# GpSimd issues the load of Wb's second quarter before its first masking product instead of after it

## The chip, the cores and the metric

The kernel runs on one core of a Trainium2 chip. The metric is the device time of one execution in microseconds (us); lower is better. A core has five engines that run their own instruction streams and wait for each other through semaphores: TensorE (PE in the profile, its weight loads PEld), VectorE (DVE), ScalarE (ACT), GpSimd (POOL) and SyncE (SP, which here only issues transfers). Data moves between the chip's memory and the on-chip buffer (SBUF) by DMA; a DMA is issued by an instruction of ACT, GpSimd or SP and then runs beside the engines. Matmul results land in PSUM, which TensorE writes and DVE and ACT read here.

## What is computed

A state-space layer (Mamba-2 in its chunked form) feeds a bilinear feed-forward layer. Batch 4, 8 heads, 768 tokens, head dimension 32, state dimension 16, all in float32 at the interface:

```python
# per batch and head, with state carried over chunks of tokens
cum = cumsum(log a)
M   = (C @ B.T) * exp(cum_i - cum_j) * causal
y   = M @ x + exp(cum_i) * (C @ state)
state = exp(sum log a) * state + sum_j exp(cum_end - cum_j) * outer(B_j, x_j)
# then, with the heads side by side: X is 3072 x 256
out = ((X @ w_a) * (X @ w_b)) @ w_out      # w_a, w_b: 256 x 1536, w_out: 1536 x 256
```

## The kernel before

The tokens are cut into 6 blocks of 128. A *pair* is two batches of one block, so there are 12 pairs (0 to 11); pairs 0 and 1 are block 0, pairs 2 and 3 block 1, and so on. One pair goes through these steps:

- B and C are scaled by decay factors (`scale_bc`, the product is at L319), giving `bm` and `cm` in float16. For pair 0, DVE does both. For pair 1, GpSimd scales B (L833) and DVE scales C (L837).
- `bm` and `cm` are transposed on TensorE, and `scores` (L427) multiplies them into four PSUM banks.
- `mask` multiplies each bank by the causal 0/1 mask and writes float16 tiles `t`. It has two forms. On DVE it is one product that reads PSUM directly (L467). With `by_pool=True`, ACT copies the bank to an SBUF tile `tmp` (L464) and GpSimd multiplies `tmp` by the mask (L465), since GpSimd works from SBUF here.
- `pv_u` (L487) multiplies the masked scores with x; ACT or DVE copy the result to float16 `X2T`.
- The feed-forward layer works on `X2T` in units of two 128-column slices of the weights: `aps` (with Wa) and `bps` (with Wb), matmuls at L667 and L682; ACT copies `aps` out (`asb`, L694), DVE multiplies it with `bps` into `hk` (L701); `ops` (L716) multiplies `hk` with Wo.

The order of instructions is written out by hand (`tc.manual_schedule()`): the order of the calls from L812 on is the order on each engine. An engine runs its own instructions in that order.

The weights are cast from float32 to float16 on the way in, by DMAs that GpSimd issues. Wa arrives in two halves, and the first half of Wb in two quarters of its own tiles, so that the first units can begin early: `load_w0(0, 0)` and `load_w0(1, 0)` bring Wa's first half and Wb's first quarter (L176, called at L232 and L233), `load_w0(1, 1)` brings Wb's second quarter (called at L859), and `load_w(1)` both second halves (L168). x of pairs 0 and 1 (`load_x0`, L151), B, C and x of pair 2 (L143), and Wo (L184) are issued by GpSimd as well. All of them share one DMA queue (q0 in the profile); SP's and ACT's transfers have queues of their own. Wb's second quarter is first read by `unit_mm(0, 1, Wb, (1,), ...)` at L898, as slices 3 to 5 of `w_of`.

GpSimd's order around the change, from the start, is: x of pair 0, Wa's first half, Wb's first quarter, x of pair 1, B of pair 1 scaled (L833), the mask of pair 0's `product0(1, 1)` (L836), Wb's second quarter, Wa's and Wb's second halves, the mask of pair 1's `product(1, 3)` (L862), three small products for the state (L864 to L866), B and C of pair 2, Wo, x of pair 2.

DVE's order beside it is: the masks of pair 0's `product0(0, 0)` and `product0(0, 1)`, C of pair 1 scaled (L837), the mask of pair 0's `product0(1, 0)`, a scan, a reciprocal, then the masks of pair 1.

TensorE's order is: scores of pair 0, warm-up matmuls, pair 1's B transposed, `pv_u(0, 0)` (heads 0 to 3 of pair 0), pair 1's C transposed, `pv_u(0, 1)` (heads 4 to 7, which read the masks of `product0(1, 0)` and `product0(1, 1)`), the scores of pair 1, and from L872 on the feed-forward units.

Of the kernel before, what the change touches and what calls it, by code (L numbers as in the profile page):

```python
# [28 lines left out]
def kernel(  # L29
# [102 lines left out]
    def by_token(t_):  # L132
        return t_.rearrange("p h r n -> p (h r n)").rearrange("p (t h n) -> p t h n", t=2, h=H)
# [31 lines left out]
    def load_w(half):  # L165
        c = slice(half * KC, (half + 1) * KC)
        return [
            nc.gpsimd.dma_start(W[half], src.rearrange("(f p) e -> p f e", p=128)[:, :, c])  # L168
            for W, src in ((Wa, moe_w_a), (Wb, moe_w_b))
        ]  # L170

    def load_w0(which, part):
        W, src = ((Wa, moe_w_a), (Wb, moe_w_b))[which]
        w = (KC, KC // 2)[which]
        t_ = W[0][part] if which else W[0]
        nc.gpsimd.dma_start(t_, src.rearrange("(f p) e -> p f e", p=128)[:, :, part * w : (part + 1) * w])  # L176
# [109 lines left out]
    def of_pair(f, blk, bp):  # L286
        if blk * NBP >= P0:
            return flat(f, blk, blk + 1).rearrange("p (b r h) -> p b r h", b=NBP, r=2)[:, bp]
        return f[:, blk, :, bp]
# [16 lines left out]
    def scale_bc(p, which, eng, factor=None):  # L306
        blk, bp = divmod(p, NBP)
        name, f = (("bm", fB), ("cm", fC))[which]
        raw = by_token(pair_in[p][which]) if p >= P0 else pair_in[p][which].rearrange("p h r n -> p r h n")
        if p >= P0 and which:  # L310
            eng.tensor_tensor(  # L311
                out=planes[p % 2][:, 4:6].rearrange("p t (h n) -> p t h n", n=N),
                in0=raw,
                in1=of_pair(f, blk, bp).unsqueeze(3).broadcast_to((128, 2, H, N)),
                op=ALU.mult,
            )
            return
        m_ = mid.tile([128, 2, H, N], f16, name=name, tag=name)
        eng.tensor_tensor(  # L319
            out=m_,  # L320
            in0=raw,
            in1=(of_pair(f, blk, bp) if factor is None else factor).unsqueeze(3).broadcast_to((128, 2, H, N)),
            op=ALU.mult,
        )
        st.setdefault(p, {})[name] = m_
        if p >= P0:
            dst = planes[p % 2][:, 0:4].rearrange("p (t e) (m f n) -> p t e m f n", e=2, f=2, n=N)
            for e in range(2):
                eng.tensor_copy(dst[:, :, e, :, e], m_.rearrange("p t (m f) n -> p t m f n", f=2)[:, :, :, e])
# [76 lines left out]
    def scores(p):  # L406
        BT, CT = st[p]["BT"], st[p]["CT"]
        st[p]["T1"] = mid.tile([128, H, 2, Q], f16, name="t1", tag="t1")
        for e, bt, m in itertools.product(range(2), range(2), range(4)) if p >= P0 else ():
            rows = slice(32 * m, 32 * m + 32)  # L410
            c0 = (e * 2 + bt) * Q
            nc.tensor.matmul(  # L412
                SC[m][:, c0 : c0 + Q],
                BT[rows, e, bt],
                CT[rows, bt],
                start=True,
                stop=True,
                skip_group_check=True,
                tile_position=(32 * m, 0),
            )  # L420
        for e in range(2) if p < P0 else ():
            for r in range(2):
                for m in range(4):
                    for bt in range(2):
                        rows = slice(32 * m, 32 * m + 32)
                        c0 = (e * 2 + r) * Q
                        nc.tensor.matmul(  # L427
                            SC[m][64 * bt : 64 * bt + 64, c0 : c0 + Q],
                            BT[rows, e, r, bt],
                            CT[rows, bt],  # L430
                            start=True,
                            stop=True,
                            skip_group_check=True,
                            tile_position=(32 * m, 64 * bt),
                        )
# [13 lines left out]
    def product0(m2, e):  # L449

        return (
            st[0]["T1"][:, 4 * m2 : 4 * m2 + 4].rearrange("p (m e) r q -> p e m (r q)", e=2)[:, e],
            (SC0, SC1)[m2][:, :, e * 256 : e * 256 + 256],
        )

    def mask(out_in, by_pool=False, by_token=False):
        o_, i_ = out_in
        if by_token:
            c_ = causal_q.unsqueeze(1).broadcast_to((128, 4, Q))
        else:  # L460
            c_ = causal.rearrange("p r q -> p (r q)").unsqueeze(1).broadcast_to((128, 2, 2 * Q))
        if by_pool:
            tmp = mid.tile([128, *c_.shape[1:]], f32, name="tmp", tag="tmp")
            nc.scalar.copy(tmp, i_)  # L464
            nc.gpsimd.tensor_tensor(out=o_, in0=tmp, in1=c_, op=ALU.mult)  # L465
        else:
            nc.vector.tensor_tensor(out=o_, in0=i_, in1=c_, op=ALU.mult)  # L467
# [363 lines left out]
    warmup(2, SC[3], 128)  # L831
    scores(0)
    scale_bc(1, 0, nc.gpsimd)  # L833
    mask(product0(0, 0))
    mask(product0(0, 1))
    mask(product0(1, 1), by_pool=True)  # L836
# [19 lines left out]
    over_mid(2, NBLK)  # L856
    raw = [lambda bt=bt: nc.scalar.mul(U32[:, 0, bt], st[0]["DS"][bt], XS) for bt in range(2)]
    raw[0]()
    load_w0(1, 1)  # L859
    w1 = load_w(1)  # L860
    scores(1)
    mask(product(1, 3), by_pool=True)  # L862
# [290 lines left out]
```

## Time and profile before

| what | value |
|---|---|
| time, median of 3 runs | 121.41 us (121.41 to 121.86) |
| the profiled execution's own time | 121.82 us |
| its span, first to last instruction | 120.1 us |
| mean granted TensorE clock | 0.997 |
| busy: TensorE | 115.1 us (96%) |
| busy: DVE, ACT, GpSimd | 86.2, 73.7, 60.6 us |

The span is what the profiler sees of the profiled execution; the time holds 1.7 us more around it. Times in the views are counted from the start of the span. A line of the timeline gives start, duration, engine, kernel line, operation, output and inputs, and in brackets for how long the engine was idle before it and what ended that idle time. The chain of work that ended last lists, from the last instruction back, what released what. An engine's busy share is an average over the whole span and says little about the first 25 us, where the change lies.

### The profile page before, as it was taken

Reading aid. Unit: us, or ns where it says so; the run is one execution under the profiler, and the core shown is the slowest. Engines: PE = TensorE matmul, PEld = TensorE weight load, DVE = VectorE, ACT = ScalarE, POOL = GpSimd, SP = SyncE. Lnnn points to the kernel's source line nnn. Section 1 sums busy time; section 2 is a strip of 40 time slices with the busy share of each in tenths; the row PEclk is TensorE's granted clock in tenths of the full one; section 3 lists DMA queues with packets and bytes.
Section 4 is the critical chain, followed back from the end, with each engine's and each line's share of the span. In section 5 each row is a group of like instructions: output and inputs, shape, how many; then the busy total and the mean of one; then the engine's idle time right before and its main releaser. Section 6 shows DMA issues by size and latency. Waiting matters only on the chain.

```text
span 120.1 us, 3705 instructions
## 1 busy us (share of the span) xinstructions
PE 115.1 (96%) x1452; PEld 80.2 (67%) x1452; DVE 86.2 (72%) x169; ACT 73.7 (61%) x151; POOL 60.6 (50%) x105
## 2 busy tenths in 40 slices
PE   5997999999999999999999999999999999999990
PEld 5645899888898888544475464765465684655890
DVE  5988785994989897599975999576899435847100
ACT  0467767676875777887567737645645737566220
POOL 6998997299978532596834992039400000000200
PEclk9999999999999999999999999999999999999998
DMA  3999999958949799579788947879601012010032
GB/s 62 146 162 155 181 202 171 228 95 104 115 79 90 128 175 93 91 123 177 76 110 153 100 167 262 115 83 180 203 0 49 11 40 81 0 49 0 20 111 87
DMA packets 69185, 13.44 MB, mean 112 GB/s; under 512 B 64048, under 2 KB 68912, under 8 KB 69168
## 3 DMA queue, kind: packets, MB, share of 16 engines
q1 hardware_dynamic: 62272, 9.31, 47.2%
q0 software_dynamic: 4368, 3.54, 18.6%
q10 hardware_dynamic: 2528, 0.36, 1.8%
q8 instruction: 11, 0.18, 0.6%
q14 instruction: 6, 0.05, 0.2%
HBM read 11.11 MB, written 3.15 MB: 119 GB/s over the span
## 4 chain that ended last, share of the span: by engine, by line
PE 82%; DMA 7%; POOL 4%; DVE 2%; ACT 1%; issue 1%
PE ops L771 18%; PE aps L746 18%; PE bps L746 17%; PE ops L716 8%; DMA Wo<-in_moe_w_out_dram 7%; PE aps L667 4%; PE bps L667 4%; PE SC L239 4%; PE SC L412 2%; PE SC L473 2%; POOL bn L143 1%; DVE t L467 1%; POOL cn L143 1%; POOL t L465 1%; PE SC L566 1%
## 5 line engine op out<-in xcount | busy, mean ns | idle before, releaser
L694 ACT COPY asb<-aps 128x512 f32<-128x512 f32 x72 | 41.4, 588 | 13.9 <-PE aps L746 9.6
L756 DVE TENSOR_TENSOR hkb<-bps,asb 128x512 f16<-128x512 f32 x48 | 32.3, 688 | 12.8 <-ACT asb L694 11.8
L746 PE MATMUL aps<-XB,Wa 128*128 128x512 f16 x96 | 28.6, 379 | 0.0
L746 PE MATMUL bps<-XB,Wb 128*128 128x512 f16 x96 | 28.5, 379 | 0.0
L771 PE MATMUL ops<-Wo,hkb 128*128 128x256 f16 (+1 forms) x204 | 22.5, 267 | 0.0
L771 PEld LDWEIGHTS <-hkb 128*128 128x128 f16 x204 | 18.5, 98 | 3.1
L467 DVE TENSOR_TENSOR t<-SC,causal_q 128x512 f16<-128x512 f32 x27 | 17.2, 681 | 3.1 <-PE SC L412 3.1
L701 DVE TENSOR_TENSOR hk<-bps,asb 128x512 f16<-128x512 f32 x24 | 15.9, 684 | 4.5 <-PE bps L667 2.2
L746 PEld LDWEIGHTS <-Wb 128*128 128x128 f16 x96 | 9.9, 103 | 10.9
L746 PEld LDWEIGHTS <-Wa 128*128 128x128 f16 x96 | 9.7, 103 | 9.1 <-issue 0.2
L783 ACT ACTIVATE osb<-ops 128x256 f32<-128x256 f32 (+1 forms) x16 | 6.0, 378 | 14.2 <-PE ops L771 14.1
L785 POOL DMA_DIRECT2D out_dram<-osb x1 | 0.6, 647 | 26.8 <-ACT osb L783 26.8
L667 PE MATMUL bps<-X2T,Wb 128*128 128x256 f16 x96 | 13.6, 273 | 0.0
L716 PE MATMUL ops<-Wo,hk 128*128 128x256 f16 x96 | 11.7, 273 | 0.1
L667 PE MATMUL aps<-X2T,Wa 128*128 128x256 f16 x80 | 11.4, 273 | 0.0
L311 POOL TENSOR_TENSOR planes<-cn,fC 128x256 f16<-128x256 f32 x8 | 5.0, 622 | 11.2 <-DMA cn<-in_C_dram 11.0
L667 PEld LDWEIGHTS <-Wb 128*128 128x128 f16 x96 | 9.7, 103 | 0.6
L716 PEld LDWEIGHTS <-hk 128*128 128x128 f16 x96 | 8.9, 98 | 1.7 <-issue 0.3
L319 POOL TENSOR_TENSOR bm<-bn,fB 128x256 f16<-128x256 f32 x11 | 6.8, 622 | 3.9 <-DMA bn<-in_B_dram 2.9
L667 PEld LDWEIGHTS <-Wa 128*128 128x128 f16 x80 | 8.1, 103 | 0.6
L304 POOL TENSOR_SCALAR x<-xn 128x512 f16<-128x512 f32 x5 | 7.5, 1492 | 1.5 <-DMA xn<-in_x_dram 1.3
L467 DVE TENSOR_TENSOR t<-SC,causal 128x512 f16<-128x512 f32 x12 | 7.7, 683 | 0.7 <-PE SC L427 0.7
(115 smaller groups left out, 130.0 us busy)
## 6 DMA issues: line engine op xcount, KB each, us to landing
out_dram<-osb SPq DMA_DIRECT2D x22, 128.0 KB, 1.8
xn<-in_x_dram SPq DMA_DIRECT2D x6, 256.0 KB, 4.1
cn<-in_C_dram SPq DMA_DIRECT2D x8, 128.0 KB, 4.2
bn<-in_B_dram SPq DMA_DIRECT2D x8, 128.0 KB, 4.6
Wa<-in_moe_w_a_dram POOLq DMA_DIRECT2D x2, 384.0 KB, 6.6
Wo<-in_moe_w_out_dram POOLq DMA_DIRECT2D x2, 384.0 KB, 7.9
xn<-in_x_dram SPq DMA_DIRECT2D x4, 128.0 KB, 3.7
Wb<-in_moe_w_b_dram POOLq DMA_DIRECT2D x2, 192.0 KB, 5.7
```

The costliest lines, as they stand in the source:

```text
L304: eng.tensor_scalar(xo, xi, XS, None, ALU.mult)
L311: eng.tensor_tensor(out=planes[p % 2][:, 4:6].rearrange("p t (h n) -> p t h n", n=N), in0=raw, in1=of_pair(f, blk, bp).unsqueeze(3).broadc ...
L319: eng.tensor_tensor(out=m_, in0=raw, in1=(of_pair(f, blk, bp) if factor is None else factor).unsqueeze(3).broadcast_to((128, 2, H, N)), op ...
L467: nc.vector.tensor_tensor(out=o_, in0=i_, in1=c_, op=ALU.mult)
L667: nc.tensor.matmul(ps[:, kk * 2 * Q : (kk + 1) * 2 * Q], w_of(W, k, f), X2T[:, p, :, f], start=(f == 0), stop=(f == 1), skip_group_check=True,
L694: (nc.vector.tensor_copy if on_dve else nc.scalar.copy)(asb, a_ps)
L701: nc.vector.tensor_tensor(out=s["hk"][:, 2 * k2 : 2 * k2 + 2, :].rearrange("p k q -> p (k q)"), in0=b_ps, in1=asb, op=ALU.mult)
L716: nc.tensor.matmul(o_ps[:, 0:d_model], hk[:, k, bt * Q : (bt + 1) * Q], Wo[:, k, :], start=(k == 0), stop=(k == NK - 1), skip_group_check= ...
L746: nc.tensor.matmul(t_, w_of(W, k, f), XB[:, blk - P0 // NBP, f].rearrange("p t j q -> p (t j q)"), start=(f == 0), stop=(f == 1), skip_gro ...
L756: return lambda: nc.vector.tensor_tensor(out=s["hk"][:, k], in0=ps[1], in1=asb, op=ALU.mult)
L771: nc.tensor.matmul(o_ps[:, 0:w], hk[:, k, c * Q : (c + 1) * Q], Wo[:, k, cs], start=(k == 0), stop=(k == NK - 1), skip_group_check=True,)
L783: nc.scalar.activation(out=o_sb[:, 0:w], in_=o_ps[:, 0:w], func=AF.Copy, scale=1.0 / (YS * YS))
```

## The change

GpSimd's instruction that issues the DMA of Wb's second quarter is moved ahead of GpSimd's first mask. The instructions are the same, and so are the order of the DMAs among themselves and the order on every other engine.

```diff
     scores(0)
     scale_bc(1, 0, nc.gpsimd)
+    load_w0(1, 1)
     mask(product0(0, 0))
     mask(product0(0, 1))
     mask(product0(1, 1), by_pool=True)
@@
     raw = [lambda bt=bt: nc.scalar.mul(U32[:, 0, bt], st[0]["DS"][bt], XS) for bt in range(2)]
     raw[0]()
-    load_w0(1, 1)
     w1 = load_w(1)
```

## The prediction

> **What bounds the kernel now.** I read the chain of waits that ended last first, then the timeline of each engine around the place of the change, then the transfers that GpSimd issues. The whole-span shares say that TensorE is busy 96% of the span; the question is therefore where TensorE still waits and what the moved instruction can do to those waits.
>
> The chain, in the stretch from the masks of pair 0 to the arrival of Wo (start, duration, what):
>
> ```profile
> 7.94 0.68 DVE t L467
> 8.62 0.80 DVE cm L319
> 9.42 0.61 DVE t L467
> 10.04 0.04 issue
> 10.08 0.39 PE py L487 x16
> ...
> 11.59 1.15 POOL t L465
> ...
> 16.94 8.62 DMA Wo<-in_moe_w_out_dram
> 25.56 0.04 issue
> 25.60 1.47 PE ops L716 x12
> ```
>
> DVE's last mask of pair 0 releases `pv_u(0, 1)` at 10.08; from there the chain goes through GpSimd's second mask and its issues to Wo, whose landing at 25.56 lets TensorE go on. Behind 25.60 the chain is TensorE to the end.
>
> TensorE's own waits in the first 27 us, after its warm-up has begun, are two short ones:
>
> ```profile
> 10.08 0.30 PE L487 MATMUL py<-t,x 64*32 64x128 f16 x16 [0.31 <-DVE t L467]
> 10.31 0.43 PE L427 MATMUL SC<-ct,bt 32*64 32x128 f16 x32
> 11.08 1.05 PE L682 MATMUL aps<-X2T,Wa 128*128 128x256 f16 x8 [0.34 <-DMA Wa<-in_moe_w_a_dram]
> ```
>
> The second, 0.34 us until Wa's first half lands, is a buffer: whatever makes `pv_u(0, 1)` late by up to 0.34 us costs nothing, since TensorE would stand there anyway. At 25.60 there is a third: TensorE is busy 0.90 us in the stretch from 25 to 26, so it loses about 0.10 us to Wo.
>
> GpSimd around the change:
>
> ```profile
> 7.35 0.62 POOL L319 TENSOR_TENSOR bm<-bn,fB 128x256 f16<-128x256 f32 x1
> 7.98 1.16 POOL L465 TENSOR_TENSOR t<-tmp,causal 128x512 f16<-128x512 f32 x1
> 9.09 0.76 POOL L176 DMA_DIRECT2D Wb<-in_moe_w_b_dram  x1
> 9.84 0.71 POOL L168 DMA_DIRECT2D Wa<-in_moe_w_a_dram  x1
> 10.54 0.72 POOL L168 DMA_DIRECT2D Wb<-in_moe_w_b_dram  x1
> 11.59 1.15 POOL L465 TENSOR_TENSOR t<-tmp,causal 128x512 f16<-128x512 f32 x1 [0.33 <-ACT tmp L464]
> ```
>
> The stream is dense from 7.35 to 11.26, then idle 0.33 us until ACT's copy for the second mask is there.
>
> DVE beside it, the two scalings of C (first pair 0's, then pair 1's) and the product after it:
>
> ```profile
> 5.36 0.42 DVE L319 TENSOR_TENSOR cm<-cn,fps 128x256 f16<-128x256 f32 x1
> ...
> 8.54 0.89 DVE L319 TENSOR_TENSOR cm<-cn,fC 128x256 f16<-128x256 f32 x1
> 9.35 0.68 DVE L467 TENSOR_TENSOR t<-SC,causal 128x512 f16<-128x512 f32 x1
> ```
>
> The reader is to see that the same operation takes 0.42 us at 5.36 and 0.89 us at 8.54, and that it ends at 9.43, 0.29 us behind the end of GpSimd's mask at 9.14. Its 256 elements need little more than that, so the trace looks as if it stood still while GpSimd's mask ran and then did its work. The earlier one ran while GpSimd only issued DMAs.
>
> **The change part by part.**
>
> *The issue goes in front.* GpSimd's `bm` ends at 7.97. An issue that follows a product starts about 0.05 us before the product's shown end (9.14 to 9.09), so this one starts at 7.92; with 0.72 to 0.76 us (the first Wb issue took 0.71) it ends at 8.64 to 8.68. The next product starts 0.01 to 0.06 us behind an issue (7.29 to 7.35 after x), so the first mask can start at 8.65 to 8.74 instead of 7.98, some 0.7 us later. Its input `tmp` is long there: ACT copies it from 7.32 to 7.91.
>
> *Who waits for that mask.* `pv_u(0, 1)` at 10.08 reads both GpSimd's mask and DVE's last one. Undisturbed, the mask ends at 8.74 + 1.16 = 9.90 at the latest, 0.18 us ahead of 10.08. So the delay of 0.7 us lies beside DVE's path, which today ends last. If that cover were gone, the same 0.7 us would stand on the path, less the 0.34 us at 11.08.
>
> *The scaling of C meets the mask differently.* DVE's `cm` can start when its mask ends at 8.62 (the row gives 8.54, as rows overlap by 0.08). The mask now starts at 8.65 to 8.74, so `cm` is first by 0.03 to 0.20 us. Then it is `cm` that runs free and the mask that stands: `cm` takes its 0.34 to 0.42 us and ends at about 8.96 to 9.04, DVE's last mask ends at 9.57 to 9.65 instead of 10.03, and GpSimd's mask runs from there: 8.96 + 1.16 = 10.12, or 10.20 with the later end. `pv_u(0, 1)` then waits for GpSimd instead of DVE and starts at 10.16 to 10.24, which is 0.08 to 0.16 us later. That is what is late next, and TensorE absorbs it at 11.08, inside its 0.34 us. Sum for TensorE: 0. [...]
>
> *DVE's scan* (0.40 us at 9.95, two SBUF inputs) could now meet the mask as well; it would end by about 10.4 to 10.5 against 10.35, and the next DVE mask waits for TensorE's scores until 10.88, so this costs nothing.
>
> *What is queued behind on GpSimd.* One mask and three issues take the same time together. With the mask ending at 10.12 to 10.20, Wa's and Wb's second halves are issued at about 10.1 and 10.85 and done by 11.6, 0.3 us later than now. GpSimd's second mask started at 11.59 when `tmp` was there; with ACT late by 0.08 to 0.16 us as well, it starts at 11.67 to 11.75. The three small products and seven issues behind it (B, C, Wo, the first x of pair 2) shift by 0.1 to 0.2 us. SP's queue and ACT's keep their order; SP's next transfers wait for Wb's second half, which landed at 10.54 + 7.9 = 18.4.
>
> *The transfers.* The order in q0 is unchanged, and the queue is backlogged: Wa's first half was issued at 4.48 and landed at 11.08, Wb's first quarter at 12.0, pair 1's x at about 12.4 and 12.9, Wb's second quarter at 9.09 + 4.7 = 13.8. TensorE first needs that quarter at 14.69, so 0.9 us of slack hides it already, and an earlier landing is worth nothing by itself. Only a gap in the queue could be closed by an earlier issue. There is one candidate, in the quarter from 11.25 to 11.5:
>
> ```profile
> q0 software_dynamic: 22, 0.02, 53.5%
> ```
>
> The share is 104% in the quarter before and 132% in the one behind, so at most about 0.2 us of queue time is missing there. Bounds: nothing if the transfers that decide a landing have no gap, and 0.2 us earlier for all that follows, Wo included, if it is closed. I take 0, because landings come 1.3 to 2 us after most of their packets, which points to a few late streams that are backlogged throughout. If Wo does land 0.2 us earlier, TensorE gains its 0.10 us at 25.60. In the other direction the issues of Wa's and Wb's second halves, 0.3 us late, have a backlog of over 2 us ahead of them, and Wo at 16.27 one of 7 to 8.6 us until landing; I cost that at 0, with 0.2 us as the upper bound.
>
> *The sum.* Against the profiled execution: 120.1 us of span, 0 from TensorE at 11.08, between -0.10 and +0.2 at 25.60, taken as 0: 120.1, and with the 1.7 us around it 121.8. That execution stands 0.4 us above the median of the runs shown, so on the median the forecast is 121.4 us, with 121.3 to 121.6 for this case.
>
> **The rivals.**
>
> *The mask gets there first (slower).* The margin of 0.03 to 0.20 us is thin, and GpSimd's start depends on issues while DVE's depends on arrivals and on TensorE's scores, so it can tip. Then `cm`, with its two SBUF inputs, stands until the mask ends, at 8.70 + 1.16 = 9.86, and needs 0.29 us more (10.15); DVE's last mask ends at 10.76 and `pv_u(0, 1)` starts at 10.80, 0.72 us late. TensorE absorbs 0.34, so 0.38 us reach the units; GpSimd's second mask ends at 13.46 instead of 12.74, and pair 1's `pv1`, now at 13.3 to 13.5, just gets it. Of the 0.38, the 0.10 lost to Wo today hide a part: +0.28. If Wo also lands later with its issue, the full 0.72 counts. Middle +0.45: 121.9 us. It passes the 0.5% mark (0.6 us) only if Wo follows its issue. For it speaks the thin margin, against it DVE's earlier row start of 8.54. [...]
>
> *The gap in the queue is closed and the path gets shorter (faster).* With `cm` free and the queue filled, the waits of 0.31, 0.34 and 0.10 us on TensorE are all there is to win: 0.75 at most, and TensorE is bound by Wo's landing, which moves by 0.2. Likely -0.1 to -0.4: 121.2 us. For it speaks the 53.5%, against it the backlog.
>
> *A new wait elsewhere (slower).* The gap on TensorE around 10 us grows, or pair 1's x, which lands at about 12.9 and is needed at 12.94, comes later because Wb's packets now stand closer behind it. Each us there is a us on the path: +0.7 or more, 122.2 us. The shared order of the queue speaks against it.
>
> **How the numbers follow.** Forecast 0.55, mask first 0.28, gap closed 0.10, new wait 0.07. A measurement of this kernel can tell about 0.5% from no change, since its three runs lie 0.4% apart. Slower by more than that: half of the second case and nearly all of the last, 0.14 + 0.06 = 0.20. Faster by more: half of the third, 0.05. The rest, 0.75, is within. The range runs from 121.0 (gap closed, most of its waits won) to 122.1 (mask first with all of its 0.72); what lies outside is some of the last case and the ends of the others, under 0.2. For the likeliest case alone it is 121.3 to 121.6.
>
> **What the profile after would show.** If the steps hold: GpSimd's issue at 7.9 and its mask behind it, DVE's `cm` near 0.42 us instead of 0.89, `pv_u(0, 1)` released by GpSimd's mask at about 10.2, TensorE still standing for Wa until about 11.1, and Wo landing near 25.6. If `cm` keeps 0.89 us or grows to 1.5, and `pv_u(0, 1)` starts near 10.8, the mask was first. If q0's share in the quarter from 11.25 is over 100% and Wo lands before 25.4, the gap was real. The prediction is wrong if TensorE's start of the units moves from 11.08, or Wo's landing by more than 0.3 us, either way.

## The result and the profile after

The changed kernel takes 123.13 us (median of 6, 122.41 to 123.33) against 121.63 us (121.15 to 122.25): ratio 1.012, 95% interval 1.009 to 1.015. It is slower by 1.2%, and outside the range of 121.0 to 122.1. The profiled execution took 123.04 us with a span of 121.3 us, 1.2 us more than before. The ratios here leave out the few executions of the kernel before that lie over 1.5% above its fastest, among them all six whose mean TensorE clock was below 0.99, so they compare with the kernel before at full clock.

The chain of waits of the changed kernel, over the stretch that the prediction showed:

```profile
7.79 0.68 DVE t L467
8.47 1.70 DVE cm L319
10.17 0.61 DVE t L467
10.78 0.04 issue
10.82 0.30 PE py L487 x16
```

DVE's scaling of C (`cm`) stands on it with 1.70 us instead of 0.80. The timelines of GpSimd and of DVE say why (start, duration, engine, line):

```profile
7.93 0.76 POOL L176 DMA_DIRECT2D Wb<-in_moe_w_b_dram  x1
8.71 1.17 POOL L465 TENSOR_TENSOR t<-tmp,causal 128x512 f16<-128x512 f32 x1
```

```profile
8.38 1.78 DVE L319 TENSOR_TENSOR cm<-cn,fC 128x256 f16<-128x256 f32 x1
10.09 0.68 DVE L467 TENSOR_TENSOR t<-SC,causal 128x512 f16<-128x512 f32 x1
```

The issue and the mask stand where the prediction put them. But the scaling, free to start at 8.47 when DVE's mask ends, is done only at 10.16, 0.28 us behind the end of GpSimd's mask at 9.88. The mask won, although its row starts 0.24 us later. TensorE:

```profile
10.22 0.28 PE L378 MATMUL SC<-ident,cm 128*128 128x128 f16 x2 [0.83 <-DVE cm L319]
10.82 0.30 PE L487 MATMUL py<-t,x 64*32 64x128 f16 x16 [0.31 <-DVE t L467]
11.06 0.43 PE L427 MATMUL SC<-ct,bt 32*64 32x128 f16 x32
11.42 1.50 PE L682 MATMUL aps<-X2T,Wa 128*128 128x256 f16 x8
12.71 1.06 PE L667 MATMUL aps<-X2T,Wa 128*128 128x256 f16 x4
...
17.00 1.92 PE L667 MATMUL bps<-X2T,Wb 128*128 128x256 f16 x16
```

and before, behind the eight matmuls at 11.08 that the prediction shows:

```profile
11.97 0.60 PE L667 MATMUL aps<-X2T,Wa 128*128 128x256 f16 x4
...
15.35 1.92 PE L667 MATMUL bps<-X2T,Wb 128*128 128x256 f16 x16
```

The units start at 11.42 instead of 11.08, 0.34 us later, and the wait for Wa is gone. The second loss is in the durations: four matmuls that took 0.60 us now show 1.06, eight that took 1.05 show 1.50. The view by stretches has the reason (length, then PE and its busy time, PEld, DVE, ACT, POOL, then the granted TensorE clock, DMA share, GB/s):

```profile
8.00:11.88 3.88, 2.70 (x99) 1.75 (x100) 3.51 (x6) 2.48 (x10) 3.25 (x4) 1.00 1.48 185
11.88:15.28 3.40, 3.40 (x63) 2.24 (x61) 2.19 (x4) 1.81 (x5) 2.78 (x6) 0.50 1.10 168
15.28:20.00 4.72, 4.72 (x46) 4.43 (x45) 3.98 (x9) 3.26 (x9) 4.72 (x8) 1.00 0.82 152
```

From 11.88 to 15.28, for 3.4 us, TensorE ran at half clock. From the start of the units to the 16 matmuls of `bps` behind them it was 11.08 to 15.35 before and is 11.42 to 17.00 now: 4.27 against 5.58 us, 1.31 us lost.

The account of the two profiled executions: +0.34 for the late start, +1.31 for the clock, -0.17 up to the `ops` matmuls at L716 (23.37 before, 24.85 after), and -0.25 inside these, since the wait for Wo is gone; that is +1.23, and the span grew by 1.2. Wo's second half landed some 6.6 us after its issue, near 24.3, where it had taken 8.6 us and landed at 25.56.

Of the six executions, five had a mean clock of 0.983 to 0.986 (123.04 to 123.33 us). The sixth had 1.000 and took 122.41 us.

### The profile page after: what moved, and what is told of

It reads as the page before. It is cut to its first block, busy times and chain, and to the rows that moved or that the text cites. A ratio compares the mean times of both kernels' runs of the same rounds, so it can differ in the third digit from the quotient of the medians.

```text
span 121.3 us, 3705 instructions
## 1 busy us (share of the span) xinstructions
PE 115.6 (95%) x1452; PEld 80.7 (66%) x1452; DVE 87.3 (72%) x169; ACT 73.5 (61%) x151; POOL 60.3 (50%) x105
## 4 chain that ended last, share of the span: by engine, by line
PE 89%; DVE 5%; DMA 2%; ACT 1%; issue 0%
PE ops L771 18%; PE aps L746 17%; PE bps L746 17%; PE ops L716 9%; PE bps L667 9%; PE aps L667 8%; PE SC L412 2%; PE aps L682 2%; PE SC L473 2%; DMA a_sb<-in_a_dram 2%; DVE t L467 1%; DVE cm L319 1%; PE SC L427 1%; PE SC L487 1%; DVE Pr L246 1%; PE SC L566 1%
## 5 line engine op out<-in xcount | busy, mean ns | idle before, releaser
L694 ACT COPY asb<-aps 128x512 f32<-128x512 f32 x72 | 41.4, 588 | 13.7 <-PE aps L746 9.6
L667 PE MATMUL bps<-X2T,Wb 128*128 128x256 f16 x96 | 14.1, 279 | 0.0
L716 PE MATMUL ops<-Wo,hk 128*128 128x256 f16 x96 | 11.5, 273 | 0.0
L716 PEld LDWEIGHTS <-hk 128*128 128x128 f16 x96 | 8.9, 98 | 1.4
L465 POOL TENSOR_TENSOR t<-tmp,causal_q 128x512 f16<-128x512 f32 x5 | 5.8, 1160 | 5.7 <-ACT tmp L464 5.6
```

What stands on the lines that cost most here:

```text
L667: nc.tensor.matmul(ps[:, kk * 2 * Q : (kk + 1) * 2 * Q], w_of(W, k, f), X2T[:, p, :, f], start=(f == 0), stop=(f == 1), skip_group_check=True,
L694: (nc.vector.tensor_copy if on_dve else nc.scalar.copy)(asb, a_ps)
L716: nc.tensor.matmul(o_ps[:, 0:d_model], hk[:, k, bt * Q : (bt + 1) * Q], Wo[:, k, :], start=(k == 0), stop=(k == NK - 1), skip_group_check= ...
```

## The experiments

The theory after this result has two steps. First, DVE's scaling of C and GpSimd's mask exclude each other, and with the issue in front the mask shuts the scaling out. Second, TensorE, which stands meanwhile, gets a lower clock behind it. The rivals are that the earlier transfer costs the time through the queue, and that the clock fell for another reason. All ratios are against the kernel before, run on the same chip; "low clock" counts executions with a mean clock below 0.99. The tile `pause`, where there is one, is written and not read. The changed kernel itself ran a second time on one chip only, beside the kernels with the late scaling and with the memset ahead of the issue; what it would have measured beside the others is not on record, so ratios from different chips are compared with care.

| run | ratio (95% interval) | low clock |
|---|---|---|
| changed kernel | 1.012 (1.009 to 1.015) | 5 of 6 |
| changed kernel, another chip | 1.011 (1.003 to 1.018) | 1 of 4 |
| changed, scaling reads PSUM | 1.004 (1.001 to 1.008) | 0 of 10 |
| the same, another chip | 1.007 (1.003 to 1.010) | 2 of 10 |
| changed, four more warm-ups | 1.001 (0.999 to 1.004) | 0 of 10 |
| changed, memset behind the issue | 1.002 (0.998 to 1.005) | 0 of 10 |
| changed, short memset behind the issue | 1.008 (1.004 to 1.012) | 0 of 5 |
| changed, memset ahead of the issue | 1.005 (1.001 to 1.010) | 1 of 8 |
| before, two warm-ups less | 1.011 (1.006 to 1.016) | 3 of 4 |
| before, scaling reads PSUM | 1.004 (1.001 to 1.008) | 0 of 10 |
| before, memset ahead of the mask | 1.005 (1.002 to 1.009) | 1 of 10 |
| before, scaling late by a DVE memset | 1.012 (1.005 to 1.019) | 1 of 4 |
| before, two more warm-ups | 0.999 (0.996 to 1.002) | 0 of 12 |
| before itself, beside the last twelve | | 6 of 83 |

### Take the collision away

```diff
-    scale_bc(1, 1, nc.vector)
+    scale_bc(1, 1, nc.vector, v.rearrange("p (r b h) -> p r b h", r=2, b=NBP)[:, :, 1])
```

> The changed kernel, but DVE's scaling of pair 1's C takes its factors from PSUM instead of from the SBUF tile fC, so that it has one SBUF input; nothing else is touched. Theory (the scaling and GpSimd's mask exclude each other, since both read two SBUF operands): the scaling falls from 1.78 us to about 0.42 us and ends near 8.9, the last mask of DVE ends near 9.5, pv_u(0, 1) starts by 10.1, the clock stays at 1.0, and the time is that of before, ratio 0.994 to 1.004. Rival (the earlier transfer itself costs the time, through the queue): the ratio stays at 1.012.

The scaling's factors now come from the PSUM bank `fps`. GpSimd's and DVE's timelines:

```profile
8.71 1.17 POOL L465 TENSOR_TENSOR t<-tmp,causal 128x512 f16<-128x512 f32 x1
```

```profile
8.49 0.41 DVE L319 TENSOR_TENSOR cm<-cn,fps 128x256 f16<-128x256 f32 x1
9.42 0.74 DVE L246 TENSOR_TENSOR_SCAN Pr<-a_sb,zero 32x128 f32<-32x128 f32 x1
```

With one SBUF input the scaling takes 0.41 us beside the same mask, so the second SBUF input is what collided. The scan with its two SBUF inputs now meets the mask instead: 0.74 us instead of 0.40, ending at 10.16, again 0.28 us behind the mask's end at 9.88. The units start at 11.04 and the clock holds in all ten executions. The ratio of 1.004 lies at the edge of what was expected and under 1.012, and something small is left.

In this profile TensorE stood once more:

```profile
13.15 0.21 PE L514 MATMUL SC<-x,bm 64*32 64x64 f16 x3
13.95 0.24 PE L514 MATMUL SC<-x,bm 64*32 64x64 f16 x13 [0.59 <-issue]
```

To see whether that and the 0.4% come from the earlier transfer, the kernel was run again beside the kernel before with the same edit:

> The changed kernel with the scaling's factors from PSUM once more, on the same chip as the kernel before with this edit; the two differ only in the place of the issue. Theory (the earlier transfer is worth nothing and costs nothing): the two ratios agree within 0.3%. Rival (the earlier transfer costs something by itself, which the ratio of 1.004 in the first run of this kernel may show): this one is 0.4% or more above the other. A second thing to see is whether TensorE stands again for about 0.6 us near 13.3 in the state's products, as in the first run; if it does not, that was one execution's.

> The kernel before with DVE's scaling of pair 1's C taking its factors from PSUM, so that it cannot collide with GpSimd's mask. It asks what the collision costs before the change, and, beside the rerun of the changed kernel with the same edit, what the earlier transfer does alone. Theory (a late scaling is absorbed while TensorE waits for Wa, as long as the clock holds): the scaling takes 0.42 instead of 0.89 us, pv_u(0, 1) starts near 9.6 instead of 10.08, the units still start near 11.1, ratio 0.997 to 1.003. Rival (the late scaling is on the path): 0.45 us gained, ratio 0.996 or below.

The ratios are 1.0065 (1.003 to 1.010) and 1.0044 (1.001 to 1.008). They differ by 0.2%, inside their intervals, so an effect of the earlier transfer alone is not shown, in either direction. Read the other way, moving the issue costs 1.1 to 1.2% where the scaling and the mask can collide, and 0.2%, which the noise covers, where they can't: the collision carries the loss. Two of the ten executions behind the 1.0065 had the low clock, so that does not vanish altogether with the collision. The stand in the state's products came back (0.60 us at 13.89), at the same instruction, and 0.35 and 0.25 us of it in two other executions of kernels with the early issue. In the profiles of before and of before with this edit the same 16 matmuls show 0.46 us instead of about 0.25, so a part of it is there too. The profile names nothing that TensorE waits for there. One thing in the traces fits: in both profiles the stand is ahead of the fourth of these matmuls, and TensorE goes on 2.2 to 2.3 us after the one 16 KB packet of the queue that the view names `q8 instruction` (at 13.95 after 11.63 in the first, at 13.89 after a packet between 11.6 and 11.7 in the second). No run tested whether the two belong together, so its cause stays open.

Before with the edit is not faster: the scaling took 0.41 us and `pv_u(0, 1)` started at 9.71, but the units waited until 11.65 for Wa in that execution. Gaining on the scaling was worth nothing there, since Wa landed behind it. That this kernel measured 0.4% slower was not expected, and the profile gives no more than that later landing for it; the 0.4% that is left with the edit in the changed kernel may be the edit's own.

### Keep TensorE busy, or less busy

```diff
     part(1)
-    warmup(2, tcp)
+    warmup(6, tcp)
```

> The changed kernel with four more warm-up matmuls of 512 columns (some 0.22 us each) on TensorE ahead of pv_u(0, 0), in time that TensorE otherwise spends waiting for the scaling of C. Theory (two costs: the late scaling, about 0.35 us at the start of the units, and on top a lower TensorE clock that follows from TensorE's longer standstill): the scaling stays at about 1.7 us, the units still start near 11.4, but the granted clock stays at 1.0 from 12 to 16; ratio 1.003 to 1.008. Rival (the lower clock has another cause than the standstill, or comes by chance): clock about 0.59 from 12 to 16 again, ratio 1.012.

In the changed kernel with this edit the collision is as before (`cm` 1.52 us, from 8.65), and TensorE's timeline starts the units as late as after the change:

```profile
11.42 1.06 PE L682 MATMUL aps<-X2T,Wa 128*128 128x256 f16 x8
12.31 0.60 PE L667 MATMUL aps<-X2T,Wa 128*128 128x256 f16 x4
```

But eight matmuls take 1.06 us, not 1.50; the clock held in all ten executions, and the ratio fell from 1.012 to 1.001 (0.999 to 1.004). Four matmuls that compute nothing took the loss away with the collision left in. By this run the clock is the larger part, and a start of the units that is 0.34 us late costs little by itself. The runs below do not all agree on the second half of that.

The other way round, the kernel before with `warmup(2, tcp)` left out:

> The kernel before without the two warm-up matmuls of 512 columns that stand ahead of pv_u(0, 0); the scaling and the mask are not touched. It asks whether TensorE standing longer between 8 and 10 is enough by itself to lower the clock. Theory: TensorE is idle some 0.4 us more in that stretch, the clock falls in at least some executions as after the change, ratio 1.004 to 1.012, with pv_u(0, 1) still at about 10.1. Rival (the clock falls for another reason): ratio 0.998 to 1.002, clock 0.997 as before.

Neither the collision nor the transfer was touched: `pv_u(0, 1)` started at 10.04. The stretches (from 7.60 to 11.00 TensorE was busy 2.65 us before):

```profile
7.60:11.00 3.40, 2.27 (x93) 1.28 (x92) 3.03 (x7) 2.40 (x11) 3.40 (x5) 1.00 1.38 174
11.00:14.34 3.34, 3.00 (x15) 2.08 (x16) 1.73 (x3) 1.66 (x4) 2.85 (x7) 0.50 1.24 168
```

The clock fell to half from 11.00 until about 14.4, three executions of four had it, and the ratio is 1.011 (1.006 to 1.016), the changed kernel's. From the start of the units to the 16 matmuls of `bps` it was 11.34 to 17.02, 5.68 us instead of 4.27. So the fall came here behind a thinner stretch of TensorE without a collision, and with it a loss of this size in that execution. The run does not divide it cleanly: the units waited for Wa until 11.34, and the one execution at full clock took 123.07 us, as long as the others and 0.8% above the 122.13 us of before at full clock.

### The late scaling alone

```diff
+    nc.vector.memset(pause.bitcast(u32), 0)
     scale_bc(1, 1, nc.vector)
```

> The kernel before with a memset of about 1.25 us on DVE ahead of the scaling of pair 1's C; GpSimd and its transfers are not touched. It makes the scaling as late as the change does (end near 10.15) without a collision and without an earlier transfer. Theory (the late scaling, and TensorE's standstill behind it, are all of the loss): pv_u(0, 1) near 10.8, units from about 11.4, the clock falls in a good part of the executions, ratio 1.005 to 1.014, as for the changed kernel. Rival (the moved transfer or the collision costs something by itself): ratio 1.000 to 1.004, clock 1.0.

The kernel before, its transfers and GpSimd's order as they were, became slower by 1.012 (1.005 to 1.019). In the profiled execution `pv_u(0, 1)` started at 11.19 and the units at 11.78; there TensorE's two warm-up matmuls ahead of `pv_u(0, 0)` also took 1.03 us instead of the 0.59 of before, so that the start is later than expected. Only one of four executions had the low clock. A late scaling is therefore enough for a loss of this size, but this run does not divide it between start and clock.

The changed kernel once more, beside it:

> The changed kernel as it is, on another chip and beside the next two, to see in how many executions the clock falls: five of the six so far had a mean clock of 0.983 to 0.986 and one had 1.000. If the fall belongs to the change: ratio 1.008 to 1.014 and at least half of the executions at 0.987 or less; if it was that chip's: clock 1.0 and ratio 1.002 to 1.007.

The loss came again, 1.011 (1.003 to 1.018), but with the low clock in one execution of four (123.73 us). The other three took 122.19, 122.41 and 123.31 us at clock 1.000, against 122.11 for the median of before at full clock on that chip. In all, 6 of 10 executions of the changed kernel had the low clock, and 6 of 83 of the kernel before. On this chip alone it was one of 4 against three of 13, so here the change did not bring the low clock more often, and with those three counted in, the medians, 122.86 and 122.18 us, are 0.6% apart. What the late start costs at full clock is not settled: these three lie 0.1 to 1.0% above that median, the run with four more warm-ups 0.1% above its own, and the run with the short memset (below) 0.8%, in which the units started at 11.59 and TensorE stood 0.35 us more at 14.4.

### Who gets there first

Why did the mask win, when its row starts 0.24 us behind the time at which the scaling could start? Four kernels put a memset, which reads no SBUF, at different places.

```diff
     scale_bc(1, 0, nc.gpsimd)
     load_w0(1, 1)
+    nc.gpsimd.memset(pause.bitcast(u32), 0)
```

> The changed kernel with a memset of about 0.55 us, which reads no SBUF, on GpSimd between the moved issue and the first mask. It asks why the scaling, whose row begins at 8.38, lost to a mask whose row begins at 8.71. If only the mask holds the scaling up, from its own start on, the scaling gets through while the memset runs: 0.4 to 0.6 us, ending by 9.1; the mask then runs from 9.3 to 10.4, pv_u(0, 1) starts near 10.5, ratio 0.998 to 1.005. If the mask holds it up from well before its row, or everything on GpSimd does, the scaling ends near 10.7 and pv_u(0, 1) starts near 11.4, ratio 1.012 or more.

> The changed kernel with the memset of 0.55 us ahead of the moved issue instead of behind it, so that the mask's row begins near 9.25 as with the memset behind it, but directly behind an issue. It asks whether a mask behind an issue shuts the scaling out from well before its row. If so, the scaling, which can begin near 8.5, ends near 10.7 and pv_u(0, 1) starts near 11.3; ratio 1.010 to 1.020. If what counts is the row's start, give or take 0.3 us, the scaling ends by 9.0 and pv_u(0, 1) starts near 10.5; ratio 0.999 to 1.006.

The first has the memset behind the issue, the second the same memset ahead of it. In both, the mask's row starts at 9.17. GpSimd's and DVE's rows with the memset behind the issue:

```profile
7.93 0.76 POOL L177 DMA_DIRECT2D Wb<-in_moe_w_b_dram  x1
8.68 0.55 POOL L836 MEMSET pause<- 128x512 uint32 x1
9.17 1.18 POOL L466 TENSOR_TENSOR t<-tmp,causal 128x512 f16<-128x512 f32 x1
```

```profile
8.41 0.41 DVE L320 TENSOR_TENSOR cm<-cn,fC 128x256 f16<-128x256 f32 x1
```

and with the memset ahead of it:

```profile
7.93 0.52 POOL L835 MEMSET pause<- 128x512 uint32 x1
8.40 0.76 POOL L177 DMA_DIRECT2D Wb<-in_moe_w_b_dram  x1
9.17 1.17 POOL L466 TENSOR_TENSOR t<-tmp,causal 128x512 f16<-128x512 f32 x1
```

```profile
8.51 2.13 DVE L320 TENSOR_TENSOR cm<-cn,fC 128x256 f16<-128x256 f32 x1
```

The mask is at the same place, and the scaling takes 0.41 us in one and 2.13 in the other. In the first the scaling ran while the issue was still under way (until 8.69), so an issue alone does not shut it out. In the second the mask was next in line behind the issue, and the scaling stood from about 8.6 on, 0.57 us ahead of the mask's row. The changed kernel is the closest comparison with the first: its issue stands at the same 7.93, its scaling could start at 8.47 instead of 8.50, and with the mask in place of the memset behind the issue it lost. So a mask that waited directly behind an issue already shut the scaling out while the issue ran. That is the step that the prediction lacked. The times, 1.002 (0.998 to 1.005) and 1.005 (1.001 to 1.010), lie in the order of the two but do not divide them; the second is lower than expected, and its clock fell in one of eight executions only.

> The kernel before with a memset of about 0.7 us on GpSimd ahead of its first mask, and the issue left behind it: the mask is late as after the change, without the transfer being earlier. Theory A (the late mask is enough, and it shuts out the scaling some 0.2 to 0.3 us ahead of its own row): mask row near 8.65, scaling to about 10.1, pv_u(0, 1) near 10.8, clock below 0.7 from 12 to 16, ratio 1.008 to 1.014. Theory B (an issue directly ahead of the mask is needed to shut the scaling out): the scaling takes 0.4 us and ends near 8.9, the mask waits for it and ends near 10.0, clock 1.0, ratio 0.998 to 1.004.

Here a memset stands where the issue would be, and the issue behind the mask. GpSimd's and DVE's rows:

```profile
8.52 1.43 POOL L466 TENSOR_TENSOR t<-tmp,causal 128x512 f16<-128x512 f32 x1
```

```profile
8.52 0.41 DVE L320 TENSOR_TENSOR cm<-cn,fC 128x256 f16<-128x256 f32 x1
```

Both rows start together, the scaling runs free, and the mask takes 1.43 instead of 1.16 us: it stood 0.27 us. This is the main case of the prediction, seen here with a memset in front instead of an issue. The ratio of 1.005 (1.002 to 1.009) is a little more than its theory B expected.

> The changed kernel with a short memset (about 0.2 us) between issue and mask instead of the 0.55 us one, so that the mask's row begins near 8.9. It measures from when on the mask shuts the scaling out. If from its own row's start, the scaling, which can begin at about 8.45 to 8.6, gets through and ends by 9.0: ratio 0.998 to 1.004. If from more than 0.3 us earlier, the scaling ends near 10.35, pv_u(0, 1) starts near 11.0 and the clock falls, ratio 1.01 or more.

GpSimd's and DVE's rows:

```profile
8.68 0.26 POOL L836 MEMSET pause<- 128x160 uint32 x1
8.87 1.18 POOL L466 TENSOR_TENSOR t<-tmp,causal 128x512 f16<-128x512 f32 x1
```

```profile
8.62 1.72 DVE L320 TENSOR_TENSOR cm<-cn,fC 128x256 f16<-128x256 f32 x1
```

With 0.26 us of memset between issue and mask (8.68 to 8.94), the mask's row starts at 8.87 and the scaling could start at 8.70; it was shut out and ended at 10.34. `pv_u(0, 1)` started at 10.99 and the ratio is 1.008 (1.004 to 1.012), without a low clock in five executions. So the mask's hold also reached ahead of its row, by 0.17 us or more, behind a memset that follows an issue, but not behind the memset of 0.55 us, where the scaling took 0.41 us. When exactly it begins is not settled.

### The kernel before with two more warm-ups

```diff
     part(1)
-    warmup(2, tcp)
+    warmup(4, tcp)
```

> The kernel before with two more warm-up matmuls of 512 columns ahead of pv_u(0, 0). Five of 66 executions of the kernel before, beside the runs so far, had a mean clock of 0.986 or less. If TensorE's short standstill near 10 is what lets the clock fall now and then, this kernel has none of these executions and otherwise the time of before: ratio 0.997 to 1.002. Rival (the warm-ups push pv_u(0, 1) back and cost their own time): units start later than 11.1, ratio 1.002 to 1.005.

In the kernel before, this gave 0.999 (0.996 to 1.002): 121.80 us against 122.15, no execution of twelve with a low clock, against one of 17. `pv_u(0, 1)` starts at 10.14 and the units at 10.94, so the warm-ups cost nothing that shows. A gain is not shown either, and none of twelve beside one of 17 does not show that the clock always holds here.

## Why the prediction was wrong

The first two parts held. The issue took its place at 7.93 (forecast 7.92), the mask started at 8.71 (8.65 to 8.74) and ended at 9.88 (9.90 at the latest).

*The step that failed* is the one titled "The scaling of C meets the mask differently": "`cm` is first by 0.03 to 0.20 us". It took the rows' starts for the order in which the two engines run. The rows do not show that: with a mask waiting behind an issue, the scaling was shut out from before the mask's row (0.57 us before it with the memset ahead of the issue). The first rival was this case and had its sizes: DVE's last mask to end at 10.76 (it ended at 10.77), `pv_u(0, 1)` at 10.80 (10.82), 0.38 us to reach the units (0.34), GpSimd's second mask to end at 13.46 (13.48). It had a chance of 0.28. Its time, 121.9 us, was still 1.2 us short of the 123.13 measured. What stood behind the failed step on GpSimd came out otherwise too: the issues of the second halves were not late (Wa's at 9.81, forecast 10.1), since the mask did not stand, and GpSimd's second mask was later (12.33, forecast 11.67 to 11.75).

That the two exclude each other was the right reading of rows that do not quite show it: the scaling at 5.36 reads `fps`, which is in PSUM, so it is not the same operation as the one at 8.54, which reads `fC` from SBUF. The row of the kernel before that has two SBUF inputs and no product on GpSimd beside it is this one, and it takes 0.42 us as well, while GpSimd issues transfers:

```profile
5.02 0.42 DVE L319 TENSOR_TENSOR bm<-bn,fB 128x256 f16<-128x256 f32 x1
```

The exclusion itself held in the runs, in both directions: the one that was shut out took longer, the scaling 1.78 us instead of 0.41 and the mask 1.43 us instead of 1.16. That the one whose row starts first runs free was the prediction's estimate, and it can't be read off the starts of rows, as the pair of runs with the mask at 9.17 shows (0.41 and 2.13 us for the scaling).

*The term that was missing* is TensorE's clock. The prediction priced a longer standstill by its length alone. The loss that followed was 1.31 us in the profiled execution, four times the late start of 0.34. The third rival named a growing gap around 10 us, but as "Each us there is a us on the path", and gave it 0.07.

Why the clock falls in some executions and not in others is not explained, and no run set it on purpose. Both falls in the profiles lasted 3.4 us: 11.88 to 15.28 in the changed kernel, and 11.00 to about 14.4 in the kernel before with two warm-ups less. In both profiles TensorE was busy 2.27 us of the 3.4 us ahead of the fall. That alone does not lower the clock. Here is the stretch from 8.47 to 11.88 of the changed kernel, of its second profiled execution, of the memset ahead of the issue and of the memset behind it:

```profile
8.47:11.88 3.41, 2.27 (x97) 1.52 (x96) 3.04 (x5) 2.38 (x10) 2.78 (x4) 1.00 1.55 187
8.47:11.88 3.41, 2.26 (x96) 1.52 (x95) 3.04 (x6) 2.37 (x10) 2.78 (x4) 1.00 1.55 187
8.47:11.88 3.41, 1.80 (x92) 1.08 (x90) 3.26 (x5) 1.92 (x8) 3.24 (x4) 1.00 1.56 186
8.47:11.88 3.41, 2.83 (x99) 1.95 (x98) 3.01 (x7) 2.75 (x11) 3.25 (x5) 1.00 1.51 183
```

Only the first was followed by a fall. The second holds a standstill of 0.84 us and the third one of 1.29 us, and behind both the clock stayed at 1.00. So neither TensorE's busy time nor its standstill in that stretch decides by itself. For the standstill speak the counts: the memset behind the issue, which has no long standstill (2.83 us busy), and the four more warm-ups had the low clock in none of ten executions each, the changed kernel in 6 of 10. Against it stand the memset ahead of the issue, with one execution of eight, and the short memset, with none of five.

The longest standstill ahead of the fall was 0.83 us in the changed kernel and about 0.3 us with two warm-ups less.

*The transfers*: "I take 0" for the queue is not contradicted, since the two kernels that differ only in the place of the issue are 0.2% apart, inside their intervals. The gap in the queue was there to be closed in that execution: q0's share in the quarter from 11.25 is 140.4% after, against 53.5%, and Wo landed before 25.4, which is the prediction's own sign for its second rival. It was worth nothing, though: Wb's second quarter, issued 1.16 us earlier, landed at 13.7 instead of 13.8. The reading of Wo's landing as a limit was wrong: 25.56 belonged to that one execution, and with the issue left in its old place it was 24.5 at the latest in the run with the late scaling (6.4 us after an issue at 18.1). The wait for it was also larger than the 0.10 us of the prediction: the `ops` matmuls at L716 took 0.25 us less without it. What the prediction let Wo absorb was not there to rely on.

## What to carry to other kernels

Before an instruction is moved ahead of another on GpSimd, look at what DVE runs beside the shifted one: here a DVE product with two SBUF inputs and a GpSimd product that reads SBUF stood in line for each other (1.78 us instead of 0.41 for DVE's, 1.43 instead of 1.16 for GpSimd's), and a start that was free 0.24 us ahead of the other's row did not tell who is first. Giving DVE's product a PSUM operand took it out of the line (0.41 us beside the same mask), though that gained no time over the kernel before (1.004). And a standstill of TensorE early in a kernel, in a stretch that is already thin, is to be priced with TensorE's clock: in one execution 0.83 us were followed by 1.3 us lost at half clock, in another 0.84 us were not, and with four warm-up matmuls in the idle time none of ten executions had that.

## What was not expected of the hardware

A GpSimd product that waits directly behind an issue on its own engine shut out a DVE instruction from 0.57 us before its row began (2.13 us instead of 0.41), while the issue alone did not. The clock of TensorE fell to half (0.50) for 3.4 us although no single standstill ahead of it was longer than 0.83 us, and the kernel before, left unchanged, had a mean clock below 0.99 in 6 of 83 executions. Landings of one transfer from execution to execution differ by more than the 0.34 us that the change moved the units: Wa's first half was there by 10.94 us in the kernel before with two more warm-ups and landed at 11.08 in the kernel before and at 11.65 in the one whose scaling reads PSUM, and none of these edits touches the transfers.
